# Four layers on one core: weight loads on another queue, TensorE transposes for the first chunk, warm-up matmuls, and new constants in the instruction scheduler

## The chip, the cores and the metric

The kernel runs on one core of one Trainium2 chip. The metric is device time in microseconds (us) of one execution. "The profile" is one execution recorded by the hardware profiler; its span is some 2 us shorter than the device time.

## The reference, cut to what matters

Four layers in turn over 2,048 tokens of width 448, in bf16, two of each kind:

```
x = x + A(layernorm(x))   # attention, 16 heads of 28, each token sees 8 tokens at stride 2
x = x + B(layernorm(x))   # feed-forward: (x @ w_gate) * (x @ w_up) @ w_down, inner width 1792
x = x + A(layernorm(x))
x = x + B(layernorm(x))
```

Both A layers share weights, and so do both B layers. The weights that A needs first are `wqkv` (1.2 MB). The output projection `wo` and the feed-forward weights are 5.2 MB and are needed later.

## The kernel before: the parts that matter

The tokens are cut into four chunks of 512 (four blocks of 128 each). A chunk is normalized on VectorE, transposed into `xnT`, and multiplied on TensorE. The program is built by a list scheduler written in Python: each operation has dependencies, a priority and an estimated duration. The scheduler simulates the engines and thus fixes, before the kernel runs, *the order of instructions on each engine*. At run time every engine works through its list in that order and waits on semaphores. A wrong estimate costs no correctness, but it can put an instruction in front of others that could have run.

```python
SEQ = "A00 A01 B10 A02 B11 A03 B12 A20 B13 A21 B30 A22 B31 A23 B32 B33".split()
                              # job = layer kind, layer, chunk: "B10" is layer 1, chunk 0
class Sched:
    PE_LAT = 205.0
    LAT = 100.0
    SAME = 60.0
# ... cut ...
def plain_dma(q, dst, src, key, sem, deps=(), lat=3000.0, prio=0.0):
    sc.add(q, one(lambda E: E.dma_start(dst, src), key), 60.0 if q == "sp" else 80.0, ...)
# ... cut: x in four chunks on SP, wqkv on the ScalarE queue ...
for j in range(4):            # output projection
    plain_dma("sp", dst, src, ("wo", j), "d_wo", deps=["c_wo"], lat=12000.0, prio=-45)
# gate, up and down weights
            plain_dma("sp", Wt[:, c, :], src[chunks[c]:chunks[c] + 128, :], (nm, c), f"d_{nm}", lat=22000.0, prio=-30)
plain_dma("sp", WD[:], ..., "wd", "d_wd", lat=30000.0, prio=-29)
# ... cut: in ln_chunk, one DMA transpose per block of 128 tokens, issued from SP ...
                sc.add("sp", one(lambda E, slot=slot, c0=c0: E.dma_start_transpose(X[:, :, c0:c0 + 128], xn_sb[:, slot, :]), ("T", li, B)),
                       70.0, deps=..., dma=f"d_t{par}_{j}", mode=li, lat=2300.0, prio=prio)
```

The number 70.0 in the last line says that the SP engine is busy for 70 ns when it issues a transpose.

The softmax here doesn't subtract the row's maximum and nothing guards it: scores larger than these inputs give would overflow.

## Time and profile before

Median 474.5 us (473.3 to 478.7 in four runs).

| what | before |
|---|---|
| span of the profile | 476.7 us |
| first matmul | 29.9 us |
| first feed-forward matmul (job B10) | 75.3 us |
| from there to the end | 401.4 us |

The first lines of the page, with the busy time of TensorE (PE) and of its weight loads, and three of its rows of 40 slices: busy tenths of PE, clock granted to PE in tenths of full speed, busy tenths of the DMA engines.

```profile
span 476.7 us, 7611 instructions
PE 415.6 (87%) x3125; PEld 170.9 (36%) x3168; DVE 245.6 (52%) x482; ACT 216.9 (46%) x346; POOL 3.9 (1%) x16
...
PE   0049767979999899979999799997999999999997
...
PEclk9999986989999999997999999998999999999999
DMA  8971013210003202020020310001011200000001
```

PE does nothing in the first two slices, while the DMA engines are full. The SP engine's part of the timeline (start, duration, instruction, count) tells why:

```profile
0.80 2.27 SPq L386 DMA_DIRECT2D x_sb<-in_A_x_dram  x4
3.12 2.59 SPq L386 DMA_DIRECT2D WG<-in_B_w_gate_dram  x3
...
9.09 12.05 SPq L386 DMA_DIRECT2D wo_g<-in_A_wo_dram  x4
21.19 17.72 SPq L479 DMA_TRANSPOSE xnTa<-xn_sb  x10
```

The ten transposes start at 21.19 us, behind all weight loads, and one occupies SP for 1.27 us at the median of the run, not for 70 ns. PE's timeline shows who waits for them. In brackets stands the idle time of PE before the row and what ended it. `WQK` marks the products for query and key ("QK matmuls" below), `WV` those for the values.

```profile
29.93 2.72 PE L499 MATMUL ps<-xnTa,WQK 128*128 128x512 bf16 x6 [29.93 <-DMA xnTa<-xn_sb]
...
100.27 1.77 PE L499 MATMUL ps<-xnTa,WQK 128*128 128x512 bf16 x6 [3.04 <-DMA xnTa<-xn_sb]
...
160.25 1.46 PE L499 MATMUL ps<-xnTa,WQK 128*128 128x512 bf16 x6 [1.25 <-DMA xnTa<-xn_sb]
...
215.09 2.42 PE L499 MATMUL ps<-WV,xnTa 128*128 128x448 bf16 x6 [3.62 <-DMA xnTa<-xn_sb]
...
271.31 2.16 PE L499 MATMUL ps<-xnTa,WQK 128*128 128x512 bf16 x6 [2.44 <-DMA xnTa<-xn_sb]
...
326.73 2.42 PE L499 MATMUL ps<-WV,xnTa 128*128 128x448 bf16 x6 [3.05 <-DMA xnTa<-xn_sb]
```

PE also has slow stretches after idle time. Two rows of the windows view, the first from a part with many short waits for VectorE and ScalarE, the second with the wait that ended at 215.09 us (stretch in us; length, busy us with instruction counts in brackets for PE, PEld, DVE, ACT and POOL; then granted clock, DMA share, GB/s):

```profile
67.10:80.80 13.70, 10.22 (x76) 3.28 (x77) 8.74 (x21) 5.57 (x11) 0.00 (x0) 0.50 0.29 59
...
214.00:220.80 6.80, 5.71 (x16) 1.69 (x18) 0.00 (x0) 0.92 (x1) 0.00 (x0) 0.50 0.07 15
```

The clock is 0.50 in both. And the whole kernel in three stretches, cut at the first matmul and at the first feed-forward matmul:

```profile
0.00:29.90 29.90, 0.00 (x0) 0.00 (x0) 8.20 (x25) 6.29 (x15) 3.91 (x16) 1.00 1.02 304
29.90:75.20 45.30, 35.87 (x406) 14.62 (x410) 30.61 (x65) 31.74 (x47) 0.00 (x0) 0.91 0.13 28
75.20:476.70 401.50, 379.71 (x2719) 156.28 (x2758) 206.78 (x394) 178.88 (x284) 0.00 (x0) 0.97 0.11 22
```

In the last stretch PE shows no work for 21.8 of 401.5 us (401.50 - 379.71), and part of the rest runs at half clock. Not all of the 21.8 us is idle time: the page has 3,125 matmuls for 3,168 weight loads, so records of 43 matmuls are missing from this trace. The waits view of the stretch (total us, times, longest) is safer. Its second line lies at least in part where records are missing:

```profile
PE ps L499 <- DMA xnTa<-xn_sb: 13.4, 5, 3.6
PE ps L499 <- issue: 5.5, 20, 2.5
```

The clock of 1.00 in the first stretch should not be read as a warm PE either. The trace has no record of half clock before 67.1 us, yet the first six matmuls (at 29.93 us) took 2.72 us, and six at 36.55 us took 1.47.

### The profile page before, as it was taken

How to read it: one execution, taken by the hardware profiler on the slowest of the kernel's cores; microseconds unless marked ns; L12 is line 12 of the kernel's file. 1: busy time of each engine (PE TensorE's matmuls, PEld its weight loads, DVE VectorE, ACT ScalarE, POOL GpSimd, SP SyncE). 2: the span in 40 equal slices, each digit the busy share in tenths (PEclk: the TensorE clock that was granted, in tenths of full speed). 3: DMA queues.
4: the chain of work that ended last, by engine and by line, in shares of the span. 5: the costliest groups of instructions: out<-in, count | busy, mean ns of one | idle time of the engine just before them, and what ended most of it. 6: DMA issues, size and time to landing. Idle time of an engine off the chain costs nothing.

```text
span 476.7 us, 7611 instructions
## 1 busy us (share of the span) xinstructions
PE 415.6 (87%) x3125; PEld 170.9 (36%) x3168; DVE 245.6 (52%) x482; ACT 216.9 (46%) x346; POOL 3.9 (1%) x16
## 2 busy tenths in 40 slices
PE   0049767979999899979999799997999999999997
PEld 0013332323444333523345233442335434335333
DVE  5135885414678637750387616851276643332342
ACT  5016883447656578223663267412673341330330
POOL 3000000000000000000000000000000000000000
PEclk9999986989999999997999999998999999999999
DMA  8971013210003202020020310001011200000001
GB/s 306 338 152 24 1 23 68 45 22 1 1 2 45 45 0 46 1 45 0 1 46 0 69 22 0 1 13 34 2 23 43 52 13 19 19 2 30 10 1 39
DMA packets 43754, 19.15 MB, mean 40 GB/s; under 512 B 35464, under 2 KB 42824, under 8 KB 43720
## 3 DMA queue, kind: packets, MB, share of 16 engines
q1 hardware_dynamic: 42568, 17.29, 15.3%
q10 hardware_dynamic: 1152, 1.38, 0.8%
q8 instruction: 25, 0.41, 0.4%
q14 instruction: 9, 0.07, 0.1%
HBM read 8.43 MB, written 1.84 MB: 22 GB/s over the span
## 4 chain that ended last, share of the span: by engine, by line
PE 82%; SPq 6%; DMA 4%; DVE 3%; issue 3%; ACT 2%; DVEq 0%
PE ps L499 43%; PE ps L744 18%; PE ps L511 9%; PE ps L689 6%; SPq L386 4%; DMA xnTa<-xn_sb 3%; PE ps L660 2%; SPq L479 2%; PE ps L637 2%; PE ps L664 1%; PE ps L538 1%; DVE hT L732 1%; DVE oT L675 1%; ACT E_sb L644 1%; DMA xnTb<-xn_sb 1%
## 5 line engine op out<-in xcount | busy, mean ns | idle before, releaser
L732 DVE TENSOR_TENSOR hT<-g_sb,ps 128x512 bf16<-128x512 bf16 x112 | 76.3, 685 | 112.6 <-ACT g_sb L729 66.8
L729 ACT ACTIVATE g_sb<-ps 128x512 bf16<-128x512 f32 x112 | 66.3, 598 | 109.4 <-PE ps L511 95.7
L499 PE MATMUL ps<-xnTb,WG 128*128 128x512 bf16 x313 | 87.4, 384 | 5.3 <-issue 4.1
L499 PE MATMUL ps<-xnTb,WU 128*128 128x512 bf16 x319 | 88.3, 381 | 1.8 <-issue 1.3
L744 PE MATMUL ps<-WD,hT 128*128 128x448 bf16 x448 | 89.3, 353 | 0.0
L499 PE MATMUL ps<-xnTa,WQK 128*128 128x512 bf16 x189 | 49.8, 402 | 37.1 <-DMA xnTa<-xn_sb 36.7
L644 ACT ACTIVATE E_sb<-ps 128x960 bf16<-128x960 f32 (+1 forms) x72 | 63.7, 926 | 28.7 <-PE ps L637 28.6
L694 DVE TENSOR_TENSOR x_sb<-x_sb,ps 128x448 bf16<-128x448 bf16 x64 | 39.5, 617 | 45.2 <-PE ps L744 32.4
L744 PEld LDWEIGHTS ps<-WD,hT 128*128 128x128 bf16 x448 | 42.8, 98 | 40.0 <-DVE st L460 0.2
L650 DVE TENSOR_TENSOR E_sb<-E_sb,MK 128x960 bf16<-128x960 bf16 (+1 forms) x72 | 44.5, 625 | 19.1 <-ACT E_sb L644 18.2
L573 ACT ACTIVATE qk<-ps 128x1024 bf16<-128x1024 f32 x29 | 29.7, 1023 | 51.1 <-PE ps L511 40.0
L499 PEld LDWEIGHTS ps<-xnTb,WU 128*128 128x128 bf16 x336 | 32.1, 98 | 38.8 <-issue 1.8
L499 PEld LDWEIGHTS ps<-xnTb,WG 128*128 128x128 bf16 x336 | 26.1, 98 | 52.1 <-issue 31.2
L460 DVE BATCH_NORM_STATS2 st<-x_sb 128x6 f32<-128x448 bf16 x64 | 39.1, 619 | 4.9 <-DMA x_sb<-in_A_x_dram 4.3
L499 PEld LDWEIGHTS ps<-xnTa,WQK 128*128 128x128 bf16 x192 | 17.3, 101 | 65.9 <-issue 44.6
L474 DVE TENSOR_SCALAR xn_sb<-x_sb,mv,rstd 128x512 bf16<-128x512 bf16 x64 | 22.4, 407 | 29.2 <-DMA xnTa<-xn_sb 19.0
L511 PE MATMUL ps<-xnTb,WT 64*128 64x512 bf16 x224 | 34.3, 385 | 0.3 <-ACT E_sb L644 0.3
L689 PE MATMUL ps<-wo_g,oT 128*128 128x448 bf16 x128 | 30.5, 367 | 2.3 <-DVE oT L675 2.2
L499 PE MATMUL ps<-WV,xnTa 128*128 128x448 bf16 x96 | 24.9, 397 | 7.3 <-DMA xnTa<-xn_sb 6.7
L619 ACT ACTIVATE v_sb<-ps 128x896 bf16<-128x896 f32 (+1 forms) x18 | 15.0, 833 | 28.9 <-PE ps L511 28.3
L669 ACT ACTIVATE R_sb<-ps 128x480 f32<-128x480 f32 (+1 forms) x36 | 19.6, 549 | 17.1 <-PE ps L660 16.7
L675 DVE TENSOR_TENSOR oT<-ps,R_sb 128x480 bf16<-128x480 f32 (+1 forms) x36 | 22.3, 625 | 8.8 <-ACT R_sb L671 4.7
(38 smaller groups left out, 175.8 us busy)
## 6 DMA issues: line engine op xcount, KB each, us to landing
x_sb<-in_A_x_dram SPq DMA_DIRECT2D x4, 448.0 KB, 7.5
out_dram<-x_sb SPq DMA_DIRECT2D x16, 112.0 KB, 1.7
WD<-in_B_w_down_dram SPq DMA_DIRECT2D x1, 1568.0 KB, 19.3
WG<-in_B_w_gate_dram SPq DMA_DIRECT2D x3, 448.0 KB, 9.7
WU<-in_B_w_up_dram SPq DMA_DIRECT2D x3, 448.0 KB, 11.6
hT<-in_A_wqkv_dram ACTq DMA_DIRECT2D x4, 224.0 KB, 4.9
xnTa<-xn_sb SPq DMA_TRANSPOSE x32, 2.5
xnTb<-xn_sb SPq DMA_TRANSPOSE x32, 2.5
```

Source lines behind the costliest of these rows:

```text
L460: sc.add("dve", one(lambda E, B=B: E.bn_stats(st6[:, B, :], x_sb[:, B, :]), ("bn", li, B)), 610.0, deps=[("x", li - 1, B)] + ([("xn", li - ...
L499: ins.append((lambda E, u=u, c=c, st=st, sp_=sp_, which=which: E.matmul(u["out"](which), u["lhs"](which, c, 0, 128), u["rhs"](which, c, 0, ...
L511: ins.append((lambda E, u=u, c=c, lo=lo, which=which, opening=opening: E.matmul(u["out"](which), u["lhs"](which, c, lo, lo + 64), u["rhs"] ...
L573: return E.activation(dst, src, ACT.Copy) if hasattr(E, "activation") else E.tensor_copy(dst, src)
L644: return E.activation(E_sb[0:nk, slot, 2 * hp:2 * hp + 2, 0:4 * nq], ps[0:nk, b0:b0 + 2, 0:4 * nq], ACT.Exp, scale=SCALE)
L650: return E.tensor_tensor(e, e, m, ALU.mult)
L675: return E.tensor_tensor(oT[:, :, tok:tok + nq], ps[:, bk[0], 0:4 * nq].rearrange("p (h n) -> p h n", h=4), R_sb[:, rs, 0:4 * nq].rearrang ...
L689: ins.append((lambda E, hc=hc: E.matmul(ps[:, bk[0], 0:D], oT[:, hc, lo:hi], wo_g[:, hc, :], start=hc == 0, stop=hc == 3), ("Y", li, B) if ...
L694: sc.add("dve", one(lambda E: E.tensor_tensor(x_sb[:, B, :], x_sb[:, B, :], ps[:, bk[0], 0:D], ALU.add), ("x", li, B)), dve_est(D), deps=[ ...
L729: sc.add("act", one(lambda E, gs=gs, bk=bk: E.activation(g_sb[:, gs, :], ps[:, bk[0], :], ACT.Copy), ("G", li, j, fc)), act_est(512), deps ...
L732: sc.add("dve", one(lambda E, gs=gs, bk=bk, fc=fc: E.tensor_tensor(hT[:, fc, hs, :], g_sb[:, gs, :], ps[:, bk[1], :], ALU.mult), ("H", li, ...
L744: ins.append((lambda E, fc=fc, bk=bk, i=i: E.matmul(ps[:, bk[0], 0:D], hT[:, fc, hs, 128 * i:128 * i + 128], WD[:, fc, :], start=fc == 0, ...
```

## The change

The intent has four parts: let the first transposes not wait behind weights (weights go to the GpSimd queue and are released when the third x chunk has landed); transpose the first chunk on PE; keep PE busy from the start so that its clock is up (20 matmuls on zeros); and give the scheduler durations that fit the chip. Cut to its core:

```diff
-DMA_T = True
+PE_T = ("00",)
+WARM = 20
 class Sched:
-    LAT = 100.0
+    LAT = 75.0
     SAME = 60.0
+    TAIL = {"pe": 0.0, "act": 125.0, "dve": 85.0, "pool": 100.0, "sp": 0.0}
@@ act_est, dve_est and other costs @@
-    return (175.0 if psum else 190.0) + 0.834 * n
+    return (50.0 if psum else 70.0) + 0.834 * n
-def dve_est(n, rate=1.0, fixed=140.0):
+def dve_est(n, rate=1.0, fixed=70.0):
@@ plain_dma @@
-        sc.add(q, ..., 60.0 if q == "sp" else 80.0, ...)
+        sc.add(q, ..., {"sp": 520.0, "act": 500.0, "pool": 1000.0}[q], ...)
@@ warm-up @@
+    for n in range(WARM):
+        sc.add("pe", one(lambda E: E.matmul(ps[:, wb[0], 0:256], warm[:, 0:128], warm[:], start=True, stop=True), ("warm", n)), 214.0, ..., prio=-100)
@@ weights @@
-    xl = [("x", -1, 15)]          # was not used
+    xl = [("x", -1, 11)]          # the third x chunk
-            plain_dma("sp", Wt[:, c, :], ...)
+            plain_dma("pool", Wt[:, c, :], ..., deps=xl, ...)   # and so for WT, WD and wo
@@ DMA transpose @@
-            if DMA_T:
+            if not by_pe:         # by_pe: layer and chunk named in PE_T
                 sc.add("sp", one(lambda E, ...: E.dma_start_transpose(...), ("T", li, B)),
-                       70.0, ..., lat=2300.0, prio=prio)
+                       1270.0, ..., lat=1500.0, prio=prio)
```

More of the change, by code (lines that the diff above doesn't have):

```diff
@@ L110, in ready_at @@
             elif src.eng == eng:
-                lat = 0.0 if eng == "pe" else self.SAME
+                lat = 0.0 if eng == "pe" else self.SAME + self.TAIL[eng]
             else:
-                lat = self.PE_LAT if src.eng == "pe" else self.LAT
+                lat = self.PE_LAT if src.eng == "pe" else self.LAT + self.TAIL[src.eng]
             r = max(r, f + lat)
@@ L223, in schedule @@
                     self.holder[b] = None
-                    self.free_at[b] = op.end
+                    self.free_at[b] = op.end + self.TAIL[op.eng]
                     key = ("rel", op.idx, b)
@@ L366, in build @@
     MK = sb([128, 2, QB], bf, "MK")
-    ident = None
-    if not DMA_T:
-        ident = sb([128, 128], bf, "ident")
+    ident = sb([128, 128], bf, "ident")
+    warm = sb([128, 256], bf, "warm")
     ps = enter(nc.psum_tensor("ps", [128, 8, 512], dt.float32))
@@ L385, in plain_dma @@
     def plain_dma(q, dst, src, key, sem, deps=(), lat=3000.0, prio=0.0):
-        sc.add(q, one(lambda E: E.dma_start(dst, src), key), 60.0 if q == "sp" else 80.0, deps=deps, dma=sem, mode=0, lat=lat, prio=prio)
+        sc.add(q, one(lambda E: E.dma_start(dst, src), key), {"sp": 520.0, "act": 500.0, "pool": 1000.0}[q], deps=deps, dma=sem, mode=0, lat=lat, prio=prio)
     for q in range(NCH):
@@ L390, in build @@
         plain_dma("sp", x_sb[:, 4 * q:4 * q + 4, :], x_par[two][:, b0:b0 + 4, :], [("x", -1, B) for B in range(4 * q, 4 * q + 4)],
-                  f"d_x{q}", lat=4000.0 + 2500.0 * q, prio=-50 + q)
+                  f"d_x{q}", lat=3300.0 + 1500.0 * q, prio=-50 + q)
     CH_ROWS = [0, 128, 192, 320]
@@ L401, in memset @@
         sc.add(eng, one(lambda E: E.memset(ap, val), key), est, prio=-40)
+    memset("dve", warm[:], 0.0, "c_warm", 100)
     memset("dve", eps_sb[:], EPS, "c_eps", 70)
+    memset("dve", wo_g[:], 0.0, "c_wo", 1000)
+    sc.add("pool", one(lambda E: E.memset(ident[:], 1.0), "i_id"), 150, prio=-46)
+    sc.add("pool", one(lambda E: E.affine_select(ident[:], ident[:], [[-1, 128]], ALU.is_equal, 0.0, base=0, channel_multiplier=1), "c_id"), 300, deps=["i_id"], prio=-46)
+    sc.add("pool", one(lambda E: E.memset(WQK[:].rearrange("p c w (h e) -> p (c w h) e", e=32)[:, :, DH:32], 0.0), "c_wqk0"), 700, prio=-45)
     memset("pool", xnT[0][:, :, 0:PAD], 0.0, "c_p0", 150)
     memset("pool", xnT[0][:, :, SEG:SEG + PAD], 0.0, "c_p1", 150)
+    memset("pool", v_sb[:, :, D:D + 32], 0.0, "c_v", 200)
     memset("pool", qk[:, :, :, 0:PAD], 0.0, "c_p2", 200)
@@ L412, in build @@
     memset("pool", ones32[:], 1.0, "c_ones", 100)
-    memset("pool", v_sb[:, :, D:D + 32], 0.0, "c_v", 200)
-    memset("pool", wo_g[:], 0.0, "c_wo", 1600)
-    sc.add("pool", one(lambda E: E.memset(WQK[:].rearrange("p c w (h e) -> p (c w h) e", e=32)[:, :, DH:32], 0.0), "c_wqk0"), 700, prio=-45)
+    wb = Banks(1)
+    for n in range(WARM):
+        sc.add("pe", one(lambda E: E.matmul(ps[:, wb[0], 0:256], warm[:, 0:128], warm[:], start=True, stop=True), ("warm", n)), 214.0, deps=["c_warm"], mode="F",
+               acquire=wb if n == 0 else None, release=[(wb, 0)] if n == WARM - 1 else [], prio=-100)
     for c in range(4):
@@ L421, in fn @@
                 return E.activation(dst, src, ACT.Copy) if hasattr(E, "activation") else E.tensor_copy(dst, src)
-            sc.add(("act", "dve"), one(fn, ("wqk", c, w)), {"act": 560.0, "dve": 330.0}, deps=[("stg", c), "c_wqk0"], prio=-28)
+            sc.add(("act", "dve"), one(fn, ("wqk", c, w)), {"act": 470.0, "dve": 330.0}, deps=[("stg", c), "c_wqk0"], prio=-28)
     WQKR = [("wqk", c, w) for c in range(4) for w in range(2)]
     WVR = [("wv", c) for c in range(4)]
-    if not DMA_T:
-        memset("pool", ident[:], 1.0, "i_id", 150)
-        sc.add("pool", one(lambda E: E.affine_select(ident[:], ident[:], [[-1, 128]], ALU.is_equal, 0.0, base=0, channel_multiplier=1), "c_id"), 300, deps=["i_id"], prio=-40)
-    xl = [("x", -1, 15)]
+    xl = [("x", -1, 11)]
+    for nm, Wt, src, chunks, tail_rows, tail_src in (("wg", WG, B_w_gate, (0, 128, 320), 64, 256), ("wu", WU, B_w_up, (0, 192, 320), 0, 128)):
+        for c in range(3):
+            plain_dma("pool", Wt[:, c, :], src[chunks[c]:chunks[c] + 128, :], (nm, c), f"d_{nm}", deps=xl, lat=12000.0, prio=-30)
+        plain_dma("pool", WT[tail_rows:tail_rows + 64, :], src[tail_src:tail_src + 64, :], (nm, 3), f"d_{nm}", deps=xl, lat=12000.0, prio=-30)
+    plain_dma("pool", WD[:], B_w_down.rearrange("(c p) e -> p c e", p=128), "wd", "d_wd", deps=xl, lat=16000.0, prio=-29)
     for j in range(4):
@@ L432, in build @@
         src = A_wo.rearrange("(c j e) d -> j e c d", c=4, j=4, e=DH)[j]
-        plain_dma("sp", dst, src, ("wo", j), "d_wo", deps=["c_wo"], lat=12000.0, prio=-45)
+        plain_dma("pool", dst, src, ("wo", j), "d_wo", deps=["c_wo"] + xl, lat=5000.0, prio=-45)
     WO = [("wo", j) for j in range(4)]
-    for nm, Wt, src, chunks, tail_rows, tail_src in (("wg", WG, B_w_gate, (0, 128, 320), 64, 256), ("wu", WU, B_w_up, (0, 192, 320), 0, 128)):
-        for c in range(3):
-            plain_dma("sp", Wt[:, c, :], src[chunks[c]:chunks[c] + 128, :], (nm, c), f"d_{nm}", lat=22000.0, prio=-30)
-        plain_dma("sp", WT[tail_rows:tail_rows + 64, :], src[tail_src:tail_src + 64, :], (nm, 3), f"d_{nm}", lat=22000.0, prio=-30)
-    plain_dma("sp", WD[:], B_w_down.rearrange("(c p) e -> p c e", p=128), "wd", "d_wd", lat=30000.0, prio=-29)
     WG_READY = [("wg", c) for c in range(4)]
@@ L459, in ln_chunk @@
         for B in range(4 * j, 4 * j + 4):
-            sc.add("dve", one(lambda E, B=B: E.bn_stats(st6[:, B, :], x_sb[:, B, :]), ("bn", li, B)), 610.0,
+            sc.add("dve", one(lambda E, B=B: E.bn_stats(st6[:, B, :], x_sb[:, B, :]), ("bn", li, B)), 525.0,
                    deps=[("x", li - 1, B)] + ([("xn", li - 1, B)] if li else []), prio=prio)
-            sc.add("dve", one(lambda E, B=B: E.bn_aggr(mv[:, B, :], st6[:, B, :]), ("mv", li, B)), 110.0, deps=[("bn", li, B)], prio=prio)
+            sc.add("dve", one(lambda E, B=B: E.bn_aggr(mv[:, B, :], st6[:, B, :]), ("mv", li, B)), 100.0, deps=[("bn", li, B)], prio=prio)
         halves = 2 if li == 0 and j == 0 else 1
+        by_pe = f"{li}{j}" in PE_T
         n = 4 // halves
@@ L467, in ln_chunk @@
             sc.add("act", one(lambda E, B0=B0, n=n: E.activation(lnv[:, B0:B0 + n].unsqueeze(2), mv[:, B0:B0 + n, 1:2], ACT.Ln, bias=eps_sb[:, 0:1], scale=1.0), ("lnv", li, B0)),
-                   230.0, deps=[("mv", li, B) for B in range(B0, B0 + n)] + ["c_eps"], prio=prio)
+                   190.0, deps=[("mv", li, B) for B in range(B0, B0 + n)] + ["c_eps"], prio=prio)
             sc.add("act", one(lambda E, B0=B0, n=n: E.activation(rstd[:, B0:B0 + n], lnv[:, B0:B0 + n], ACT.Exp, scale=-0.5), [("rstd", li, B) for B in range(B0, B0 + n)]),
-                   230.0, deps=[("lnv", li, B0)], prio=prio)
+                   165.0, deps=[("lnv", li, B0)], prio=prio)
         for B in range(4 * j, 4 * j + 4):
-            slot, prev = ring("xn", ("T", li, B) if DMA_T else ("Tps", li, B))
+            slot, prev = ring("xn", ("T", li, B) if not by_pe else ("Tps", li, B))
             src = _dup_view(x_sb[:, B, 0:256])
             sc.add("dve", one(lambda E, B=B, slot=slot, src=src: E.tensor_scalar(xn_sb[:, slot, :].rearrange("p (a n) -> p a n", a=2), src, mv[:, B, 0:1], rstd[:, B:B + 1], ALU.subtract, ALU.mult), ("xn", li, B)),
-                   300.0, deps=[("rstd", li, B), ("mv", li, B), ("x", li - 1, B), prev], prio=prio)
+                   325.0, deps=[("rstd", li, B), ("mv", li, B), ("x", li - 1, B), prev], prio=prio)
             war = (readersA if par == 0 else readersB).get((li - 2, B), [])
             c0 = col(128 * B)
-            if DMA_T:
+            if not by_pe:
                 sc.add("sp", one(lambda E, slot=slot, c0=c0: E.dma_start_transpose(X[:, :, c0:c0 + 128], xn_sb[:, slot, :]), ("T", li, B)),
-                       70.0, deps=[("xn", li, B)] + war + ([f"c_p0", "c_p1"] if par == 0 else []), dma=f"d_t{par}_{j}", mode=li, lat=2300.0, prio=prio)
+                       1270.0, deps=[("xn", li, B)] + war + ([f"c_p0", "c_p1"] if par == 0 else []), dma=f"d_t{par}_{j}", mode=li, lat=1500.0, prio=prio)
             else:
@@ L487, in ln_chunk, with ft @@
                 sc.add("pe", ins, 4 * 56.0, deps=[("xn", li, B), "c_id"], mode="F", acquire=bk, prio=prio)
-                sc.add("act", one(lambda E, c0=c0, bk=bk: E.activation(X[:, :, c0:c0 + 128], ps[:, bk[0], :].bitcast(bf)[:, 0:512].rearrange("p (c n) -> p c n", c=4), ACT.Copy), ("T", li, B)),
-                       act_est(512), deps=[("Tps", li, B)] + war, release=[(bk, 0)], prio=prio)
+                def ft(E, c0=c0, bk=bk):
+                    src = ps[:, bk[0], :].bitcast(bf)[:, 0:512].rearrange("p (c n) -> p c n", c=4)
+                    dst = X[:, :, c0:c0 + 128]
+                    return E.activation(dst, src, ACT.Copy) if hasattr(E, "activation") else E.tensor_copy(dst, src)
+                sc.add(("act", "dve"), one(ft, ("T", li, B)), {"act": act_est(512), "dve": dve_est(512)}, deps=[("Tps", li, B)] + war, release=[(bk, 0)], prio=prio)
     def paired(tag, li, j, first, second, tdeps, prio):
@@ L650, in fm @@
                 return E.tensor_tensor(e, e, m, ALU.mult)
-            sc.add("dve", one(fm, ("E", li, qb, hp)), dve_est(8 * nq, 2.0, 90.0), deps=[("Ex", li, qb, hp), "c_mk"], prio=prio)
+            sc.add("dve", one(fm, ("E", li, qb, hp)), dve_est(8 * nq, 2.0, 60.0), deps=[("Ex", li, qb, hp), "c_mk"], prio=prio)
         return slot
```

## The prediction

> **What bounds the kernel now.** The page gives PE 415.6 us busy of a 476.7 us span; the chain of waits is 82% PE. To win: PE idle (61 us) and PE work at half clock:
>
> 1. Start. The waits view shows one PE wait of 29.9 us, for the DMA transposes of the first normalized chunk. The timeline shows why: the chunk is normalized at 10.3 us and the weights repacked at 10.8 us, but the SP queue first issues 5.2 MB of later weights and sits in the output-weight loads from 9.09 to 21.19 us. DMA share is full until 28 us.
> 2. Five later PE waits for transposed chunks (at 100, 160, 215, 271, 326 us: 3.0, 1.3, 3.6, 2.4, 3.1, sum 13.4 us). The scheduler model gave an SP transpose issue 70 ns; the trace shows 1.27 us. So PE's fixed order meets the data too early, though feed-forward work was available.
> 3. Half clock. The windows view shows a granted clock of 0.50 from 67 to 81, 101 to 105, 214 to 221 and 272 to 275 us, after idle. PE was busy 23 us in these: about 11 us lost (estimate). The first 3 us after 29.9 us are cold too (453 ns per matmul against 225 soon after): 1.5 us.
>
> **What the change does.**
> - SP has only the x loads ahead of the transposes; the weights go on the GpSimd queue once the third x chunk has landed, needed 20 to 45 us later. "DMA: Bandwidth & Descriptors" of the Trainium skill (section "Issuing engines are not separate DMA queues"): queues share the 16 DMA engines, so order is gained, not bandwidth. The second chunk's transposes will compete with the weights: landing in 4 to 7 us instead of 2.5, nearly covered by the first chunk's 11.5 us on PE.
> - First chunk by 16 PE transposes and four PSUM copies of about 0.6 us on ACT and DVE, pushing the last weight repack to 12 us. First real matmul at 12.3 us: 17.5 us saved, all critical.
> - Warm-up: 20 matmuls, 4.3 us from 1 us on. They end near 5.5 us. The skill's "TensorE: Matmul & The Clock Gate" (section "Part 1: The HAM clock gate") gives an idle window of about 3.4 us for falling back to half clock; the gap here is near 6 us. I expect cold QK matmuls still: gain 0.
> - Recalibrated model: the instruction order shows 51, 51 and 48 feed-forward matmuls ahead of the waits for transposes that had 35, 29 and 35 (215, 271, 326 us); at 0.22 us each that covers these waits. The one at 160 us gets fewer (32, was 42) and may grow by 2 us. Net: 9 us idle and 5 us half clock won, 4 us lost: 10 us.
>
> 475.2 - 17.5 - 10 = 447.7; I say 447 us, range 437 to 458. Faster by over 2%: 0.96, within: 0.03, slower: 0.01.
>
> **Right or wrong:** first QK matmul at 11.5 to 14 us; clock 0.5 there; later PE waits for transposes under 6 us in sum (13.4 before); half-clock stretches at 215 and 272 us gone; the stretch before the first feed-forward block stays at half clock, 17 us earlier.
>
> **What would make it wrong:** GpSimd descriptor generation held up, weights landing late (a wait for output weights near 36 us); the second chunk's transposes starved by the weights, a wait over 3 us near 23 us; new waits elsewhere from the new order; warm-ups holding the clock after all.

## The result, and the profile after

Median 455.7 us (455.3 to 456.5), against 474.5 us before. The ratio is 0.959, with a 95% interval of 0.953 to 0.965. Ratios here are the mean time of one kernel's runs over that of the other's of the same rounds, so they are not quite the ratio of the quoted medians. All outputs are right.

So the kernel is 19 us faster. The same views show where that came from. First the page:

```profile
span 453.6 us, 7740 instructions
PE 421.1 (93%) x3204; PEld 173.1 (38%) x3204; DVE 244.1 (54%) x484; ACT 222.6 (49%) x350; POOL 11.1 (2%) x30
...
PE   5814877999999999999999999999999999999997
...
PEclk9765995999999999999999999999999999999999
DMA  8896002410002210010020310020020201001001
```

From the eighth slice on PE is full and at full clock. The first seven slices are not good: the fourth shows PE at 4 tenths with a clock of 5 tenths. PE's and SP's timelines there:

```profile
1.13 4.45 PE L422 MATMUL ps<-warm 128*128 128x256 bf16 x20 [1.13 <-DVE eps_sb L402]
8.87 0.72 PE L490 MATMUL ps<-ident,xn_sb 128*128 128x128 bf16 x8 [3.29 <-DVE xn_sb L479]
...
12.77 2.74 PE L507 MATMUL ps<-xnTa,WQK 128*128 128x512 bf16 x6 [1.29 <-ACT WQK L429]
...
39.70 2.72 PE L507 MATMUL ps<-xnTa,WQK 128*128 128x512 bf16 x6 [15.30 <-DMA xnTa<-xn_sb]
...
153.34 1.46 PE L507 MATMUL ps<-xnTa,WQK 128*128 128x512 bf16 x6 [0.16 <-DMA xnTa<-xn_sb]
```

```profile
0.81 2.34 SPq L387 DMA_DIRECT2D x_sb<-in_A_x_dram  x4
14.58 28.02 SPq L484 DMA_TRANSPOSE xnTa<-xn_sb  x6
```

The first real matmul is at 12.77 us, 17 us earlier than before. Then PE works on the first chunk, and at 24.4 us it stands still for 15.30 us: the second chunk's transposes have not landed. The view of the transpose line, for those issued between 14 and 20 us, gives count, durations on SP, and the times from issue to landing (minimum, median, maximum):

```profile
L484 SPq DMA_TRANSPOSE xnTa<-xn_sb x4: 1271/1796/14180, 14.6 to 19.6; - x4
...
DMA to landing us min/median/max: 13.4/20.8/22.8
```

Elsewhere in the run the median landing time is 2.5 us. Everything after the second chunk is pushed back. The windows view, cut at the same events:

```profile
12.70:39.70 27.00, 11.64 (x65) 4.11 (x66) 6.05 (x22) 8.84 (x15) 6.42 (x11) 0.69 1.01 211
39.70:77.80 38.10, 30.59 (x392) 12.31 (x393) 29.10 (x57) 26.24 (x40) 0.00 (x0) 0.81 0.11 22
77.80:453.60 375.80, 372.70 (x2713) 152.56 (x2711) 200.88 (x383) 180.80 (x281) 0.00 (x0) 1.00 0.11 23
```

The first feed-forward matmul comes at 77.9 us, **2.6 us later** than before. All of the gain, and more, lies behind it: 375.8 us where the kernel before took 401.5. There PE shows no work for 3.1 us instead of 21.8 us (with missing records in the 21.8, as said), and the clock is 1.00 instead of 0.97. The five waits for transposes, 13.4 us, have shrunk to one of 0.16 us.

So the three parts of the change that work on the start had won 17 us at the first matmul and lost them, and 2.6 us more, by the first feed-forward matmul. This is a reading of one profile. The experiments test it.

### The profile page after: what moved, and what is told of

Its sections match the earlier page's. It is cut to its first block, busy times and chain, and to the rows that moved or that the text cites. A ratio compares the mean times of both kernels' runs of the same rounds, so it can differ in the third digit from the quotient of the medians.

```text
span 453.6 us, 7740 instructions
## 1 busy us (share of the span) xinstructions
PE 421.1 (93%) x3204; PEld 173.1 (38%) x3204; DVE 244.1 (54%) x484; ACT 222.6 (49%) x350; POOL 11.1 (2%) x30
## 3 DMA queue, kind: packets, MB, share of 16 engines
q0 software_dynamic: 1152, 5.22, 4.6%
q10 hardware_dynamic: 1152, 1.38, 0.9%
## 4 chain that ended last, share of the span: by engine, by line
PE 84%; DVE 6%; DMA 6%; ACT 1%; issue 0%; SPq 0%; DVEq 0%
PE ps L507 45%; PE ps L752 19%; PE ps L519 9%; PE ps L697 5%; DMA xnTa<-xn_sb 5%; PE ps L668 2%; PE ps L645 2%; DVE st L464 2%; DMA x_sb<-in_A_x_dram 1%; PE ps L672 1%; DVE oT L683 1%; DVE E_sb L658 1%; PE ps L546 1%; DVE x_sb L702 1%; DVE xn_sb L479 1%; DVE qk L581 1%
## 5 line engine op out<-in xcount | busy, mean ns | idle before, releaser
L507 PE MATMUL ps<-xnTb,WG 128*128 128x512 bf16 x336 | 91.3, 380 | 0.0
L507 PE MATMUL ps<-xnTb,WU 128*128 128x512 bf16 x336 | 90.9, 379 | 0.0
L752 PE MATMUL ps<-WD,hT 128*128 128x448 bf16 x448 | 90.5, 353 | 0.0
L507 PE MATMUL ps<-xnTa,WQK 128*128 128x512 bf16 x192 | 49.8, 397 | 16.7 <-DMA xnTa<-xn_sb 15.5
L702 DVE TENSOR_TENSOR x_sb<-x_sb,ps 128x448 bf16<-128x448 bf16 x64 | 39.2, 614 | 36.4 <-PE ps L752 26.2
L697 PE MATMUL ps<-wo_g,oT 128*128 128x448 bf16 x128 | 31.9, 379 | 4.4 <-DVE oT L683 4.3
L683 DVE TENSOR_TENSOR oT<-ps,R_sb 128x480 bf16<-128x480 f32 (+1 forms) x36 | 22.5, 626 | 15.1 <-ACT R_sb L679 11.8
L627 ACT ACTIVATE v_sb<-ps 128x896 bf16<-128x896 f32 (+1 forms) x20 | 16.8, 842 | 12.8 <-PE ps L519 12.2
L679 ACT ACTIVATE R_sb<-R_sb 128x480 f32<-128x480 f32 (+1 forms) x36 | 21.0, 583 | 0.9
## 6 DMA issues: line engine op xcount, KB each, us to landing
WU<-in_B_w_up_dram POOLq DMA_DIRECT2D x3, 448.0 KB, 11.8
```

What stands on the lines that cost most here:

```text
L507: ins.append((lambda E, u=u, c=c, st=st, sp_=sp_, which=which: E.matmul(u["out"](which), u["lhs"](which, c, 0, 128), u["rhs"](which, c, 0, ...
L683: return E.tensor_tensor(oT[:, :, tok:tok + nq], ps[:, bk[0], 0:4 * nq].rearrange("p (h n) -> p h n", h=4), R_sb[:, rs, 0:4 * nq].rearrang ...
L697: ins.append((lambda E, hc=hc: E.matmul(ps[:, bk[0], 0:D], oT[:, hc, lo:hi], wo_g[:, hc, :], start=hc == 0, stop=hc == 3), ("Y", li, B) if ...
L702: sc.add("dve", one(lambda E: E.tensor_tensor(x_sb[:, B, :], x_sb[:, B, :], ps[:, bk[0], 0:D], ALU.add), ("x", li, B)), dve_est(D), deps=[ ...
L752: ins.append((lambda E, fc=fc, bk=bk, i=i: E.matmul(ps[:, bk[0], 0:D], hT[:, fc, hs, 128 * i:128 * i + 128], WD[:, fc, :], start=fc == 0, ...
```

## The experiments

Theory A: the new scheduler constants, above all the one for the transposes, bring the gain in the long second part; the new start brings nothing net, since the second chunk's transposes compete with the weights for the DMA engines. Rival R: the early start is worth most of the gain. Each run was timed in three rounds beside the kernel before, unless said otherwise.

### e1: the changed kernel with the old constants

All scheduler constants of the diff set back, except the estimated landing times of the weights; queue, PE transposes and warm-ups stay. One dependency was added: the copies of the PE transposes into `xnTa` did not depend on the two memsets of its padding, which the new order happens to cover.

```diff
-    LAT = 75.0        # and all the other constants
+    LAT = 100.0
-... deps=[("Tps", li, B)] + war, ...
+... deps=[("Tps", li, B)] + war + ["c_p0", "c_p1"], ...
```

> The changed kernel with the scheduler model's constants set back to the old ones (and one missing dependency on two memsets added, which the new order happens not to need). Queue move, PE transposes and warm-ups stay. Theory A (the new start gives nothing net, because the second chunk's transposes starve beside the weight loads; the whole gain is the new order in the steady state): 472 to 482 us, five PE waits for transposes of 1 to 4 us back at the later chunks. Rival R (the earlier start is worth most of the gain and the order little): 454 to 464 us.

Measured: 469.75 us, ratio 0.984 (0.979 to 0.989). It is 2 us below the expected band and 6 us above the rival's. The five later waits are back (3.0, 1.2, 2.5, 2.4 and 2.6 us). The start also has a 12.4 us wait for the second chunk. The part from the first feed-forward matmul to the end takes 396.8 us, so the gain there does need the constants. But that the new start gives nothing, as theory A has it, does not hold under the old constants: this kernel is 7 us faster than the kernel before in the same rounds (median 476.9), and its first feed-forward matmul comes at 71.1 us instead of 75.3. The last of the weights landed at 33.6 us here and at 38.9 us in the change, though their issue began at 11.4 and 10.9 us. Why was not looked into.

### e2: the kernel before with only the new constants

Here too the estimated landing times of the weights are not touched; they stay as in the kernel before.

> The kernel before with only the scheduler model's constants changed; weights stay on the SP queue, all transposes on the DMA, no warm-ups. Theory A: the steady state from the first feed-forward matmul to the end takes about 376 us as in the changed kernel (401 before), the start is no later than before (first feed-forward matmul at 71 to 76 us), so 445 to 454 us, as fast as or faster than the whole change. Rival R: 466 to 475 us.

Measured: 451.14 us, ratio 0.947 (0.941 to 0.953). The constants alone, on the old queue and without PE transposes, gave a faster kernel than the whole change did (455.7). The second part takes 375.8 us. The first matmul comes at 25.8 us instead of 29.9, since the new costs also put the down-projection's weights behind the first eight transposes on SP.

### e3: weights released later

The one line that releases the weights, with everything else as in the changed kernel; the order on PE is identical.

```diff
-    xl = [("x", -1, 11)]      # third x chunk landed
+    xl = [("T", 0, 7)]        # second chunk's transposes landed
```

> The changed kernel, with the weight loads on the GpSimd queue released when the second chunk's four transposes have landed, instead of when the third x chunk has. The instruction order on TensorE is identical. Theory A (transposes starve only because weight packets share the DMA engines): each of the four lands within 4 us, the 15.3 us PE wait is under 2 us, the half-clock stretch from 26 to 43 us is gone, all later work comes 14 to 18 us earlier: 437 to 442 us. Rival S (the transposes are slow for another reason, as the SP queue or DMA write path after start-up): wait stays over 8 us. Rival T (the weights then come too late and make a new wait at the output projection or the first feed-forward block): above 446 us.

Measured: 439.74 us (439.4 to 440.1), ratio 0.922 (0.917 to 0.926), 16 us faster than the changed kernel. The same view of the second chunk's transposes, then PE's row for its first matmuls and the last stretch of the windows view:

```profile
L484 SPq DMA_TRANSPOSE xnTa<-xn_sb x4: 1248/1264/1299, 15.3 to 19.2; - x4
...
DMA to landing us min/median/max: 2.5/2.5/2.5
```

```profile
25.72 1.24 PE L507 MATMUL ps<-xnTa,WQK 128*128 128x512 bf16 x5 [0.16 <-issue]
```

```profile
61.80:437.70 375.90, 369.09 (x2675) 152.56 (x2710) 200.29 (x382) 180.71 (x281) 0.00 (x0) 1.00 0.11 23
```

All four land in 2.5 us (two later ones, beside the weights, took 6.7 and 7.1), the wait is gone, and the first feed-forward matmul comes at 61.8 us instead of 77.9. No wait for weights appears in their place: rival T falls, and rival S with it. (The 369.09 us of PE work is too low: 2,675 matmuls stand beside 2,710 weight loads, so 35 records are missing.)

### e4: the second chunk on PE too

```diff
-PE_T = ("00",)
+PE_T = ("00", "01")
```

> The changed kernel with the second chunk transposed on PE as well, weights released as in the changed kernel. Theory A: no DMA transpose is needed before about 45 us, the 15.3 us wait is gone, 437 to 444 us; the two transposes of the third chunk still land slowly (over 8 us), which costs nothing. Rival S/T: above 450 us, with another wait in its place near 25 us.

Measured: 440.58 us, ratio 0.923 (0.919 to 0.928). The 15.3 us wait is gone here too, though the weights are released as early as in the change. Only two DMA transposes now meet the weights. They still take 12.5 and 11.8 us to land, and nothing waits for them. Two different ways around the collision give nearly the same time.

### e5 and e6: the warm-up matmuls, on the kernel of e3

```diff
-WARM = 20
+WARM = 1        # e5;   e6: WARM = 54, each estimated at 148 ns
```

> The deferred-weights kernel (439.7 us) with 1 warm-up matmul instead of 20. Theory W0 (the 20 warm-ups end at 5.1 us, the clock falls back to half before the first QK matmul at 13.4 us in any case, so they are worth nothing): 438.5 to 441 us, first QK matmuls at half clock (about 450 ns each) as with 20. Rival W1 (they hold something of the clock): slower by 1.5 us or more.

Measured: 439.0 us, ratio 0.923 (0.920 to 0.926): the same as with 20. The first six QK matmuls take 2.74 us in both.

> The deferred-weights kernel with 54 warm-up matmuls, which at full clock last until about 9 us, when the first transposes can start. Theory W0: with no idle gap over 1.5 us ahead of the first QK matmul the clock stays full, the 10.2 us half-clock stretch (7 to 17 us in the deferred kernel) is gone, first QK matmuls at about 225 ns each: 1.5 to 2.5 us faster than 439.7 us, so 437 to 438.5. If the transposes do not count as activity, the clock falls all the same and the time is 439 to 441 us.

Measured: 438.57 us, but from 435.9 to 441.3 in four runs, ratio 0.921 (0.916 to 0.926). This is inconclusive. PE's timeline shows what the profiled run did:

```profile
1.13 8.90 PE L422 MATMUL ps<-warm 128*128 128x256 bf16 x54 [1.13 <-DVE eps_sb L402]
9.87 0.61 PE L490 MATMUL ps<-ident,xn_sb 128*128 128x128 bf16 x8
11.48 0.72 PE L490 MATMUL ps<-ident,xn_sb 128*128 128x128 bf16 x8 [1.00 <-DVE xn_sb L479]
13.27 2.27 PE L507 MATMUL ps<-xnTa,WQK 128*128 128x512 bf16 x6 [1.07 <-ACT WQK L429]
```

The transposes ran warm (0.61 us for eight, against 1.03 in e3 and e5), but the records of the granted clock have it fall to half at 13.8 us for 3.4 us, half a microsecond after the real work begins. The warm-ups had ended at 10.0 us, 3.8 us before. Between them and the real work lie 3.2 us, of which 16 short transposes fill 1.3. The clock was lost all the same. Whether a denser filling would hold it was not tried.

### e7: weights back on the SP queue

The changed kernel with `plain_dma("sp", ...)` for the weights and no release condition; the order on PE is the same.

```diff
-            plain_dma("pool", Wt[:, c, :], ..., deps=xl, ...)
+            plain_dma("sp", Wt[:, c, :], ..., deps=[], ...)      # and so for WT, WD and wo
```

> The changed kernel with the weight loads back on the SP queue ahead of the transposes, as in the kernel before (PE transposes of the first chunk, warm-ups and new model stay; the TensorE order is the same). Theory A: on one queue the second chunk's transposes wait behind all weights but then land fast (2.5 us each), at about 30 us, as the first chunk's did in the kernel before; the PE wait before the second chunk is 4 to 7 us instead of 15.3 us and the time 443 to 449 us, so the move to the GpSimd queue as released in the change costs 7 to 12 us. Rival (the queue move is what makes the start early): 456 us or more.

Measured: 448.48 us, ratio 0.942 (0.939 to 0.946). The PE wait is 7.8 us, a little more than expected, and the first feed-forward matmul comes at 70.7 us. The second chunk's transposes:

```profile
L484 SPq DMA_TRANSPOSE xnTa<-xn_sb x4: 1267/2062/9750, 15.0 to 29.0; - x4
...
DMA to landing us min/median/max: 3.1/5.9/15.6
```

They did not land in 2.5 us each, as expected, but in 15.6, 6.3, 5.5 and 3.1 us. The first goes out at 15.0 us, about when it does in the change (14.6). In both kernels most of the transposes get through only when the weights do: here the down-projection's weights land at 30.2 us and the transposes at 30.7 to 32.2; in the change those weights land at 38.9 us, the first transpose at 28.0 and the other three at 38.7 to 39.6. The weights are issued from 3.3 us on here, and from 10.9 us on in the change. So the move to the GpSimd queue, as released in the change, cost 7 us (455.7 - 448.5); queue and release were changed together. The 7.6 us by which the weights are released later is of that size, but it was not tested alone.

### e8: weights on the ScalarE queue (one look)

To tell "another queue" from "the GpSimd queue", the weights were issued from ScalarE's hardware queue at about the same time.

```diff
-    xl = [("x", -1, 11)]
+    xl = [("rstd", 0, 7)]                        # second chunk's statistics done, on ScalarE
-            plain_dma("pool", Wt[:, c, :], ...)
+            plain_dma("act", Wt[:, c, :], ...)     # model cost 20 ns, so that the order stays
```

> The changed kernel with the weights issued from the ScalarE hardware queue at about 13.5 us (one look; ScalarE is blocked by issuing for 6 us or more, so only the landing times of the second chunk's transposes count; one dependency on two memsets added). Theory A (any weight stream on another queue that shares the DMA engines slows the transposes, which move 256-byte packets): each of the four lands in 8 us or more. Rival G (it is something of the GpSimd queue alone): each lands in 5 us or less. Variant P (what counts is the packet beside it: 3,584 bytes on the hardware queue, 7,168 on the GpSimd one): about half of the 20 us, 8 to 12 us.

Measured: 450.66 us in a single run of unknown state. The view of the second chunk's transposes:

```profile
L484 SPq DMA_TRANSPOSE xnTa<-xn_sb x4: 1253/1350/1535, 15.3 to 19.6; - x4
...
DMA to landing us min/median/max: 4.5/11.1/15.1
```

They landed in 4.5, 8.6, 13.5 and 15.1 us. Rival G, that only the GpSimd queue does it, falls, although the first transpose, at 4.5 us, is below the 8 us that theory A had for each. Beside the weights on either of the two other queues the transposes slow down, though more beside the GpSimd queue (13.4 to 22.8). Here the last of them landed at 34.7 us, before the last weights (39.9). Variant P fits this loosely: the profiles have 5.22 MB in 1,152 packets on the GpSimd queue and 5.24 MB in 3,375 on ScalarE's (counted from 10 to 45 us). But the weights also started 3.5 us later in e8, so the packet size is argued, not shown.

### e9 and e10: which constants

e9 is the kernel before with two numbers changed; e10 is the kernel before with all the new constants but those of SP and of the DMA.

```diff
 # e9, the DMA transpose
-                       70.0, ..., lat=2300.0, prio=prio)
+                       1270.0, ..., lat=1500.0, prio=prio)
```

> The kernel before with one change in the scheduler model: a DMA transpose costs the SP queue 1270 ns to issue and 1500 ns to land, where it was 70 and 2300. Theory M (this constant is what the steady-state gain comes from): the five PE waits for transposes after the start, 13.4 us in sum before, are under 4 us, the half-clock stretches after them gone, 452 to 461 us. Rival N (the latencies and the costs of ScalarE and VectorE are what matters): 467 to 476 us.

> The complement on the kernel before: all other constants of the new model (latencies, tails, costs of ScalarE and VectorE), but SP's transpose still at 70 ns. Theory M: PE still meets the transposes too early (35 feed-forward matmuls ahead of the waits at the chunks where the new model puts 48 to 51): waits of 2 to 4 us at three to five chunks, 466 to 476 us. Rival N: 450 to 461 us.

Measured: e9 456.76 us, ratio 0.957 (0.954 to 0.960). e10 478.69 us, ratio 1.004 (1.000 to 1.008), a little above its band. PE's first line in the waits view (total us, times, longest) of e9, then of e10:

```profile
PE ps L499 <- DMA xnTa<-xn_sb: 31.0, 2, 30.4
```

```profile
PE ps L500 <- DMA xnTa<-xn_sb: 47.1, 6, 32.0
```

Taking off the first wait at the start, e9 has one wait of 0.6 us left and e10 five with 15.1 us in sum; the kernel before had 13.4. Telling the scheduler what a transpose costs on SP (its time on SP and its landing time after that, changed together) gives on its own as much as the whole change. How far off the old numbers were can be estimated: by them a chunk's four transposes are through 4 x 0.07 + 2.3 = 2.6 us after the first is issued. In the profile of the kernel before, those issued from 153.8 to 157.7 us were through at 160.1, after 6.3 us. So PE could come up to 3.7 us too early, and the five waits are 1.25 to 3.62 us. The new numbers give 4 x 1.27 + 1.5 = 6.6 us. All the other engine costs and latencies, without it, give nothing. With it they seem to add a further 5 us: e2 has 451.1 against 456.8 in e9. But e2 also has the new costs of plain DMAs, which move its first matmul, and most of its lead over e9 lies before the first feed-forward matmul (72.2 against 77.4 us; the rest is 375.8 against 377.7).

### e11: the first chunk by DMA, on the kernel of e3

```diff
-PE_T = ("00",)
+PE_T = ()
```

> The deferred-weights kernel with the first chunk transposed by the DMA as well (no PE transposes; warm-ups stay). What the PE transposes are worth once the queue is free: four SP issues of 1.27 us from 9.3 us on and 2.5 us to land put the first QK matmul at 16.5 to 18 us instead of 13.4; the second chunk's transposes land near 23 us, in time. So 3 to 5 us slower than the deferred kernel: 442 to 445 us. If the first chunk's PE transposes are needed for most of the early start, 450 us or more.

Measured: 441.31 us, ratio 0.926 (0.922 to 0.929). The first QK matmul comes at 15.9 us instead of 13.35. Once nothing stands in the way of the transposes, doing them on PE is worth 1.6 us, less than expected.

### All in two numbers

From the profiles: the first feed-forward matmul, and the time from it to the end of the span.

| kernel | first feed-forward matmul, us | rest, us | median, us |
|---|---|---|---|
| before | 75.3 | 401.4 | 474.5 |
| the change | 77.9 | 375.7 | 455.7 |
| e1 change, old constants | 71.1 | 396.8 | 469.8 |
| e2 before, new constants | 72.2 | 375.8 | 451.1 |
| e3 change, weights later | 61.8 | 375.9 | 439.7 |
| e4 change, two chunks on PE | 62.3 | 376.7 | 440.6 |
| e5 as e3, 1 warm-up | 61.1 | 376.1 | 439.0 |
| e6 as e3, 54 warm-ups | 60.6 | 377.1 | 438.6 |
| e7 change, weights on SP | 70.7 | 375.8 | 448.5 |
| e8 change, weights on ScalarE's queue (one look) | 72.9 | 376.0 | 450.7 |
| e9 before, transpose cost | 77.4 | 377.7 | 456.8 |
| e10 before, other costs | 78.2 | 399.3 | 478.7 |
| e11 as e3, no PE transposes | 64.0 | 375.6 | 441.3 |

The rest is about 376 us in every kernel whose scheduler knows what a transpose costs on SP, and 397 to 401 us in every kernel whose scheduler does not. The first column depends on what the first two chunks' transposes have to compete with.

## Why the prediction was right or wrong

The time fell in the range of 437 to 458 us and the direction was right, but that the sum was right was luck: two of its terms were wrong in opposite directions.

- **"17.5 us saved, all critical": the saving did not last.** The first matmul came at 12.77 us, as said (12.3). By the first feed-forward matmul the gain was -2.6 us. The step that failed is "landing in 4 to 7 us instead of 2.5, nearly covered by the first chunk's 11.5 us on PE". The transposes landed in 13.4 to 22.8 us and left a 15.3 us wait. The prediction had named this as a way to be wrong ("the second chunk's transposes starved by the weights"), but had put 4 to 7 us on it. It does not say where these come from; in the kernel before, the first four transposes landed in 3.8 to 7.1 us, on *one* queue with the weights and issued from 21.2 us on, when the gate and up weights were through (the last at 21.4) and the down-projection's (27.7) were not. e3 and e4 removed the collision in two ways and got 16 and 15 us back. e8 shows that it does not need GpSimd's queue, and e7 that weights ahead on the same queue hold the transposes as well.
- **"order is gained, not bandwidth": half right.** "DMA: Bandwidth & Descriptors" of the Trainium skill (section "Issuing engines are not separate DMA queues") says that the queues interleave on the same engines, and the DMA row and the 1.01 DMA share after agree. But order was lost as well as gained. On one queue, in e2, the first chunk's transposes landed at 24.2 to 25.7 us, right after the weights issued ahead of them (the last at 23.8), and the down-projection's weights, issued behind them, at 36.4. Across queues the transposes shared with the weights. The same page, section "Queues, rings and completion order", has each DMA engine take turns between queues packet by packet. That would fit transposes of about 240 bytes a packet (0.52 MB in the 2,176 packets by which the profiles of the change and of e4 differ) beside weights of 4.5 KB a packet (5.22 MB in 1,152). But no run shows the turns themselves, nor that what the profile counts as a packet is the page's packet.
- **Recalibrated model, "10 us": too small.** The mechanism was right, and e9 shows it on its own. The term measured 25.7 us (401.4 - 375.7). The waits for transposes in that part fell from 13.4 to 0.2 us. The half-clock stretches there, 22.6 us before with PE busy for 21.2 of them, went too, which is worth about half of the 21.2 (an estimate). The two make some 24 of the 25.7 us. The prediction had won "9 us idle and 5 us half clock" and lost 4. It expected the wait at 160 us to grow, since fewer feed-forward matmuls stood ahead of it; that wait is 0.16 us now. Counting one kind of matmul ahead of a wait was a poor measure, probably because other work stands there too and the transposes themselves moved; this was not traced.
- **Warm-up, "gain 0": right** (e5). The skill's "TensorE: Matmul & The Clock Gate" (section "Part 1: The HAM clock gate") has an idle window of about 3.4 us; the warm-ups left a gap of 3.3 us and then short transposes, the trace has the clock at half from 9.5 us on, 3.9 us after the warm-ups, and the first six QK matmuls took 2.72 us before and 2.74 after.
- **The signs: mixed.** First QK matmul, its half clock, and the vanished half-clock stretches at 215 and 272 us came as said. Of "later PE waits for transposes under 6 us in sum (13.4 before)", the five waits that made up the 13.4 us are down to 0.2, but with the second chunk's new wait the sum is 15.5 us. The stretch before the first feed-forward block stays at half clock, but not "17 us earlier".

In the two profiles the change thus is a gain of 26 us after the first feed-forward matmul, from the scheduler constants, and a loss of about 3 us before it. That makes 23 us, against 19 between the medians, because the profiled run of the kernel before was one of its slow ones (478.4 us). Nor do the parts of the change simply add up: the new start gained 7 us with the old constants (e1), but with the new ones it lost 5 us (455.7 against 451.1 in e2). The kernel of e3 has both gains: 439.7 us, against 455.7 and 474.5. What remains open is why the new start does better with the old constants, why the GpSimd queue slows the transposes more than ScalarE's, and what in e2 beyond the transpose cost gives its last 5 us.

## What to carry to other kernels

Where a program fixes the instruction order from a cost model, look first for the one cost that is wrong by a factor (here 70 ns for 1.27 us), and compare it with durations in the trace; it was worth more than all the refinements. Moving bulk loads to another queue does not put them behind small urgent transfers but beside them, and ahead on the same queue they hold them too: release them by a dependency on those transfers. And judge a change to the start at a later common event, not at the first matmul.

## What the Trainium skill lacked or had wrong

- "DMA: Bandwidth & Descriptors", section "Issuing engines are not separate DMA queues": it says that issuing from several engines only saves issue time. It lacks the warning that a small transfer can lose by it: with 5.2 MB of weights on another queue four transposes of 128x512 bf16 took 13.4 to 22.8 us to land (GpSimd queue) or 4.5 to 15.1 us (ScalarE queue), against 2.5 us alone.
- The same page gives no time for which a transpose of this size occupies the issuing engine: 1.27 us on SP at the median here, up to 14.2 us while the DMA engines were full. Its one table of sequencer time for DMA transposes is for other sizes.
- "TensorE: Matmul & The Clock Gate", section "Part 4: PE-mode transpose", says that transposes do not count as activity as matmuls do. e6 fits that: the clock fell 3.8 us after 54 dense matmuls although 16 transposes ran in between. It does not prove it, since they filled only 1.3 of the 3.2 us before the real work. The transposes themselves did run faster at full clock, 0.61 us for eight against 1.03 us at half clock in e3.
